# Top-1 expert layers behind attention: what an expert's rows beyond full tiles of 128 are divided into

## The chip, the cores and the metric

One core of a Trainium2 chip. The metric is the device time of one execution in microseconds (us).

## The reference, cut to what matters

```python
# attention: B=4, H=8, S=576, D=64, with a bias from a small network on log(1+|i-j|)/log(i)
x = attn_out.transpose(0, 2, 1, 3).reshape(2304, 512)
logits = normed(x) @ normed(expert_emb).T / tau          # 8 experts
expert_idx = argmax(logits, axis=1)
gate_w = softmax(logits)[arange(2304), expert_idx]
for e in range(8):                                       # F = 1024
    mask = expert_idx == e
    h = maximum(x[mask] @ w1[e], 0.0)
    out[mask] = gate_w[mask, None] * (h @ w2[e])
```

Which rows go to which expert is known only when attention is done, and the experts get very different numbers of rows.

## The kernel before, in words

**Three stages.** Attention runs in 72 units to about 400 us of the span, and each finished tile of 128 rows (18 in all) is routed and written to `xs` in HBM. Then `dispatch` (L1074) plans which rows lie where. Then `moe` (L1273) runs the expert layers.

**Slots.** The expert layers work on slots of 128 rows. A full slot belongs to one expert. What an expert has beyond full slots is rounded up to one part of 64 rows (`half`) or to a full slot, and two 64-row parts of two experts share a slot. Slots 0 to 7 (`EA`) are full ones that `early_slots` (L932) chooses when 15 of the 18 tiles are routed; the rest is planned in `dispatch`: DVE computes counts, prefix sums and comparisons on small tiles, and PE turns them into lists of row numbers (L1135 for full slots, L1160 for 64-row parts). The lists drive GpSimd's indirect DMAs: gather of a slot's rows from `xs` (L1024 early, L1314 later) and scatter of its results (L1303).

**Two programs.** `tc.If` (L1449) chooses by the number of slots used: 21 slots with 3 shared ones (`VAR`, L31), or 22 with 4.

**Expert layers.** F is cut into four quarters q of 256. The first layer of a slot and quarter (`l1`, L1342) is 12 products of 256 columns (f16 high and low halves), the second (`l2`, L1380) 6 products of 512 columns. `product` (L1295) is one matmul with a weight address from a register (the expert's number times its stride) in a full slot (L1298); in a shared slot it is two, on 64 of the array's 128 columns each, L1298 and L1300. Their second expert's weights are copied by DVE beforehand into `wx` (`second`, L1286, L1292), one copy for each layer, quarter and shared slot. ACT and DVE evict the first layer into pairs of slots `h` (three pair buffers), SP transposes a pair into `ht` (L1358), and DVE adds the second layer into `macc` (L1390; L1388 in the first quarter). Weights for the next quarter are loaded (L1246), squared for a scale (ACT L1259, PE L1236) and split into f16 halves (ACT or DVE L1264, DVE L1265) during the layer that doesn't use them; there is one copy of each layer's weights in SBUF.

**Early slots.** The first quarter's first layer of slots 0 to 7 runs inside `dispatch` (`early_x`, `early_h`). `early_act` (L1043) evicts the pairs to the last four slots' rows of `macc`, and four transposes (`early_t`, L1053, issued at L1310) take them to `ht`. A slot whose rows hold such a pair is gathered only after the transpose (token `hr`).

**Order.** `Sched` (L119) simulates engines with a cost for each operation and emits the operations in the order of their simulated starts, each engine in that order. Costs and priorities stand in the `S.op` calls: first layer `100 q + i` in the order of slots (L1283: early, four full ones, shared, the others), second layer `100 q + 21.9 + i`, weights at fractions between. The two programs are planned apart. `dispatch` is written out by hand.

Of the kernel before, what the change touches and what calls it, by code (L numbers as in the profile page):

```python
# [12 lines left out]
I32 = mybir.dt.int32  # L13
# [11 lines left out]
NM = 4  # L25
EXPM = 0x7F800000
# [4 lines left out]
VAR = (21, 3)  # L31
# [225 lines left out]
class Kern:  # L257
# [12 lines left out]
    def setup(self):  # L270
# [34 lines left out]
        self.rc = t("rcst", 293)  # L305
# [4 lines left out]
        self.oh, self.ohs, self.rh = t("oh", NT, E, dt=F16), t("ohs", NT + 1, E, dt=F16), t("rh", NT)  # L310
# [466 lines left out]
    def finish(self, pr, c, xt, prio):  # L777
# [134 lines left out]
        def take():  # L912
# [5 lines left out]
            v.scalar_tensor_tensor(g(6), self.rh[:, ts], -128.0, g(5), ALU.mult, ALU.add)  # L918
            for b in range(nb):
                v.tensor_scalar(self.opt[:, t0 + b], self.iop, g(6)[:, b:b + 1], self.tok[:, t0 + b:t0 + b + 1], ALU.is_equal, ALU.mult)  # L920
# [11 lines left out]
    def early_slots(self, prio):  # L932
# [8 lines left out]
        T = self.early = {a: t("e" + a, *sh, dt=dt) for a, sh, dt in (("cl", [E + 1], F32), ("c", [E], F32), ("be", [n], F32), ("ce", [n], F32), ("es", [EA], F32), ("esi", [EA], I32))}  # L941

        T["ni"], T["f"], T["bt"] = t("ni", E, dt=I32), t("full", E, dt=I32), t("bt", 2, E, E)[:, 0]
        T["tb"], T["os"], T["ge"] = t("tb", NT, E)[:, 0:n], t("os", NT, NB, dt=F16)[:, 0:n, 0:EA], t("ge", NB, E + 1)[:, 0:EA]
# [3 lines left out]
        def init():  # L948
            nc.gpsimd.memset(T["cl"][:, 0:1], 0.0)
            nc.gpsimd.memset(t("base", 2, E + 1)[:, :, 0:1], 0.0)  # L950

# [4 lines left out]
        op("POOL", 130, init, [], [("e", 0)])  # L956
# [38 lines left out]
        def experts():  # L995
# [3 lines left out]
            v.tensor_tensor(self.ohslot[:, 0:EA], T["ge"][:, :, 0:E], T["ge"][:, :, 1:E + 1], ALU.subtract)  # L999

# [42 lines left out]
    def early_act(self, k, part=None):  # L1043
# [3 lines left out]
        pair = lambda k: self.row[:, NS - 1 - k, 0:DM].bitcast(F16).rearrange("p (s d) -> p s d", s=2)  # L1047
# [26 lines left out]
    def dispatch(self):  # L1074
# [19 lines left out]
        full = t("full", E, dt=I32)  # L1094
        ni, fh, bt, base, rj = t("ni", E, dt=I32), t("fh", 2, E, dt=I32), t("bt", 2, E, E), t("base", 2, E + 1), t("rj", 32)
# [7 lines left out]
        v.tensor_scalar(ni, ps[:, 0:E], 63.0, None, ALU.add)  # L1103
# [3 lines left out]
        v.tensor_tensor(more, full, self.early["c"], ALU.subtract)  # L1107
        v.scalar_tensor_tensor(g(6), self.rh[:, l:l + 1], -128.0, g(5), ALU.mult, ALU.add)
# [5 lines left out]
        fsum, hsum, rests = base[:, 0, 1:E + 1], base[:, 1, 1:E + 1], base[:, 1, E:E + 1]  # L1114
# [79 lines left out]
        for k in range(2, EB // 2):  # L1194
            self.early_act(k)
# [273 lines left out]
```

## Time and profile before

| | |
|---|---|
| Median of 3 runs | 685.93 us (684.45 to 686.23) |
| Profiled execution | 688.79 us, span 686.9 us |
| Busy: PE / PE weight load | 619.5 us (90%) / 412.2 us (60%) |
| Busy: DVE / ACT / POOL | 557.7 (81%) / 471.0 (69%) / 174.1 us (25%) |
| DMA | 123.99 MB, mean 181 GB/s |
| Scatters of results (L1303) | 21, POOL, 20.9 us |

The span runs from the first to the last recorded work; the time of the execution is 1.9 us longer. Busy shares are averages over three stages. A matmul's recorded duration includes the pipeline behind its last column, so consecutive matmuls overlap in the records, and the distance between starts is what each costs.

### The profile page before, as it was taken

The page shows a single profiled execution, that of the slowest core. Times are in us where ns is not written, and L with a number is a line of the kernel's source. Part 1 is how long each engine was busy: PE and PEld are TensorE (multiplying, and loading weights), DVE is VectorE, ACT ScalarE, POOL GpSimd, SP SyncE. Part 2 cuts the span into 40 slices and gives each one's busy share as a digit, 9 for nine tenths or more (in the row PEclk, how much of TensorE's full clock was granted, in tenths as well). Part 3 has the DMA queues.
Part 4 walks back from the last instruction along what each step waited for, and adds up shares of the span by engine and source line. Part 5 has one row for each costly group of instructions (what it writes and reads, how often), then busy time and mean ns, then how long its engine had stood idle before and what let it go on. Part 6 is the DMA issues. An engine that isn't in the chain of part 4 may idle for free.

```text
span 686.9 us, 18631 instructions
## 1 busy us (share of the span) xinstructions
PE 619.5 (90%) x6356; PEld 412.2 (60%) x6356; DVE 557.7 (81%) x1573; ACT 471.0 (69%) x1056; POOL 174.1 (25%) x274
## 2 busy tenths in 40 slices
PE   6689999988999888999999877979999999999993
PEld 2345555654667667767677655854675477457641
DVE  6988898888779998999987765948789968987762
ACT  5667687877879887989998446837476647647400
POOL 3555656452221222211210164200000000000073
PEclk9799999999999999999999998989999999999997
DMA  8767646835689946986865459976399549747542
GB/s 247 225 181 218 208 143 188 236 124 164 194 186 278 226 125 153 177 214 190 199 185 130 155 128 268 213 131 194 79 234 218 157 126 233 196 128 162 127 179 100
DMA packets 147842, 123.99 MB, mean 181 GB/s; under 512 B 93830, under 2 KB 122758, under 8 KB 147744
## 3 DMA queue, kind: packets, MB, share of 16 engines
q1 hardware_dynamic: 140256, 96.87, 57.0%
q0 software_dynamic: 7488, 25.85, 11.8%
q8 instruction: 58, 0.95, 0.6%
q14 instruction: 40, 0.33, 0.2%
HBM read 80.70 MB, written 22.29 MB: 150 GB/s over the span
## 4 chain that ended last, share of the span: by engine, by line
PE 37%; issue 35%; DVE 13%; ACT 6%; POOL 4%; DMA 3%; SPq 1%; POOLq 0%; DVEq 0%; ACTq 0%
PE o L737 11%; PE s L685 7%; PE t L716 7%; PE m L630 6%; POOL out L1303 3%; DVE ss L699 3%; ACT pp L702 2%; DVE khl L514 2%; PE o L742 1%; PE m L716 1%; DMA bsc<-stg 1%; DMA macc<-xs,kept 1%; ACT pts L722 1%; PE e L1041 1%; ACT stg L643 1%
## 5 line engine op out<-in xcount | busy, mean ns | idle before, releaser
L1298 PE MATMUL p<-w1s,mxt 128*128 (+1 forms) x912 | 120.2, 276 | 0.1
L702 ACT ACTIVATE pp<-ss,mx 128x576 f32<-128x576 f32 x144 | 112.3, 782 | 11.2 <-DVE mx L699 11.2
L1298 PE MATMUL p<-w2s,mht 128*128 (+1 forms) x504 | 113.9, 379 | 2.7 <-DVE macc L1390 2.4
L699 DVE CUSTOM_DVE_ANT_0 ss<-s,bt 128x576 f32<-128x576 f32 x144 | 104.3, 752 | 11.1 <-PE s L685 9.4
L737 PE MATMUL o<-pts,v 128*64 128x128 f32 x1600 | 105.7, 278 | 3.0 <-DVE xt L754 1.9
L1298 PEld LDWEIGHTS <-mxt 128*128 128x128 f16 (+1 forms) x912 | 88.8, 100 | 24.1 <-issue 3.0
L737 PEld LDWEIGHTS o<-pts,v 128*64 128x64 f32 x1600 | 86.7, 137 | 19.6 <-issue 8.5
L716 PE MATMUL t<-ident,pp 128*128 128x128 f32 x576 | 86.7, 280 | 1.2 <-ACT pp L702 0.4
L1298 PEld LDWEIGHTS <-mht 128*128 128x128 f16 (+1 forms) x504 | 48.7, 99 | 61.4 <-issue 10.4
L685 PE MATMUL s<-kt,qt 64*128 64x512 f16 (+3 forms) x960 | 77.7, 288 | 3.9 <-DVE mx L699 3.0
L1259 ACT ACTIVATE junk<-raw 128x1024 bf16<-128x1024 f32 x50 | 52.7, 1055 | 37.5 <-DMA raw<-in_moe_w 15.7
L722 ACT COPY pts<-t 128x512 f32<-128x512 f32 x121 | 68.1, 589 | 14.0 <-PE t L716 12.6
L1303 POOL DMA_INDIRECT out<-macc,kept x21 | 20.9, 996 | 214.4 <-DVE macc L1390 214.1
L716 PEld LDWEIGHTS t<-ident,pp 128*128 128x128 f32 x576 | 63.5, 141 | 17.6 <-issue 10.0
L617 DVE TENSOR_SCALAR hid<-L,thr 128x576 f32<-128x576 f32 x128 | 65.9, 574 | 9.6 <-PE m L630 9.0
L685 PEld LDWEIGHTS <-qt 64*128 64x128 f16 (+1 forms) x960 | 40.0, 97 | 47.8 <-issue 20.7
L1390 DVE SCALAR_TENSOR_TENSOR macc<-p,aux,macc 128x512 f32<-128x512 f32 x63 | 46.8, 753 | 14.7 <-PE p L1298 13.3
L630 PE MATMUL m<-hid,wt 128*32 128x320 f32 (+1 forms) x488 | 45.3, 423 | 8.7 <-ACT stg L643 3.4
L1352 ACT ACTIVATE h<-p 128x256 f16<-128x256 f32 x70 | 26.0, 378 | 39.0 <-PE p L1298 20.9
L643 ACT ACTIVATE stg<-m,corr 128x256 f32<-128x256 f32 (+1 forms) x88 | 33.7, 418 | 23.5 <-PE m L630 18.9
L1265 DVE SCALAR_TENSOR_TENSOR w1s<-raw,wz,w1s 128x1024 f16<-128x1024 f32 x32 | 40.8, 1278 | 0.1
L1353 DVE SCALAR_TENSOR_TENSOR h<-p,h 128x256 f16<-128x256 f32 x76 | 31.8, 421 | 10.3 <-ACT h L1352 9.8
(323 smaller groups left out, 1046.9 us busy)
## 6 DMA issues: line engine op xcount, KB each, us to landing
raw<-in_moe_w SPq DMA_DIRECT2D x60, 512.0 KB, 4.0
bt<-bsc SPq DMA_DIRECT2D x64, 320.0 KB, 3.5
bsc<-stg POOLq DMA_DIRECT2D x34, 320.0 KB, 3.7
bt<-bsc SPq DMA_DIRECT2D x32, 160.0 KB, 3.4
xs<-row POOLq DMA_DIRECT2D x16, 256.5 KB, 5.6
v<-in_v SPq DMA_DIRECT2D x8, 512.0 KB, 5.4
kr<-in_k SPq DMA_DIRECT2D x8, 512.0 KB, 5.8
q<-in_q SPq DMA_DIRECT2D x8, 512.0 KB, 6.5
```

Source lines behind the costliest of these rows:

```text
L617: e.tensor_scalar(hid(), src[:, off:off + S_], self.thr[:, t0 + x:t0 + x + 1], None, ALU.max)
L630: nc.tensor.matmul(m()[32 * x:32 * x + 32, 0:n], w(x), hx[x]()[:, a:a + n], start=True, stop=True, tile_position=(0, 32 * x))
L685: nc.tensor.matmul(out, lq, k, start=xq + xk == 0, stop=xq == 1, tile_position=(64 * b, 0 if c < 4 else 64 * b))
L699: nc.vector.tensor_tensor_reduce(out=sx(), in0=ss[b]()[:, 448 * b:448 * b + S_], in1=bt()[:, 64 - 64 * b:640 - 64 * b], scale=1.0, scalar= ...
L702: nc.scalar.activation(pp()[:, S_ * b:S_ * b + S_], sx(), AF.Exp, bias=mx()[:, b:b + 1], scale=-1.0, accum_out=sums()[:, h, b:b + 1])
L716: nc.tensor.transpose(t()[:, 128 * k:128 * k + 128], pp()[:, lo + 128 * k:lo + 128 * k + 128], self.ident)
L722: (e.copy if e is nc.scalar else e.tensor_copy)(pts()[:, at:at + n].rearrange("p a b -> p (a b)"), t()[:, 0:128 * n])
L737: nc.tensor.matmul(ob()[64 * b:64 * b + 64, k:k + 128], vv[:, 8 + b if j == 4 else 4 * b + j, :], pts()[:, pb, :], start=j == 0, stop=j == ...
L1259: S.op([("ACT", 1230, lambda: nc.scalar.activation(out() if not own else dst(0), rv() if own else raw(), AF.Square, scale=2.0 ** (-8 if wh ...
L1298: nc.tensor.matmul(out[c, 0:n], lhs[:, c], w[:, bass.ds(ev[s] + at, n)], start=start, stop=stop)
L1303: ins = nc.gpsimd.indirect_dma_start(self.out, bass.IndirectOffsetOnAxis(ap=self.sidx[:, s:s + 1], axis=0), acc[:, s, :], None, bounds_che ...
L1390: S.op([("DVE", 750, lambda a=a, r=r, p2=p2: v.scalar_tensor_tensor(a, p2(), r, a, ALU.mult, ALU.add))], [("p2", q, s), ("rs", q)], [("acc ...
```

## The change

An expert's rest is now a part of 32 rows, always there, and a part of 64 rows where the rest is over 32 (rests over 96 get a full slot). 64-row parts: up to four, in two shared slots, as before. 32-row parts: eight, one for each expert, in two slots of four parts whose experts are fixed (expert 4 s + x at columns 32 x). Slots: 8 early, 2 shared, 2 fixed, 8 others, 20 in all (`NU`). A product in a fixed slot is four matmuls on 32 columns each, with weight addresses known when the program is built, and needs no copy of weights. The early pairs 0 to 2 lie in `ht` at places 8 to 13, no longer in `macc`; only pair 3 lies in the rows of slot 21. If there are more than 8 other slots or more than four 64-row parts, the else-branch computes the former plan anew (`general`) and runs 22 slots.

```diff
-VAR = (21, 3)
+NF = 8
+NU = 8 + NM + NF
...
     def early_act(self, k, part=None):
-        pair = lambda k: self.row[:, NS - 1 - k, 0:DM].bitcast(F16).rearrange("p (s d) -> p s d", s=2)
+        pair = lambda k: (self.ht[:, EB + 2 * k:EB + 2 * k + 2].rearrange("p s b t -> p (s b t)") if k < 3 else self.row[:, NS - 1, 0:DM].bitcast(F16)).rearrange("p (s d) -> p s d", s=2)
...
     def dispatch(self):
-        v.tensor_scalar(ni, ps[:, 0:E], 63.0, None, ALU.add)
+        v.tensor_scalar(ni, ps[:, 0:E], 31.0, None, ALU.add)
...
-        gm, vb, at, hh, thr = t("gm", E), t("vb", E), t("at", E, dt=I32), t("hh", 1), t("thr", E + 1)
-        v.scalar_tensor_tensor(gm, full, -1.25, half, ALU.add, ALU.add)
-        v.tensor_scalar(hh, rests, 0.5, None, ALU.mult)
-        v.tensor_tensor(vb, fsum, hsum, ALU.add)
-        v.tensor_scalar(thr, base[:, 0], hh, None, ALU.add)
-        v.scalar_tensor_tensor(at, vb, hh, gm, ALU.add, ALU.subtract)
+        v.tensor_tensor(at, base[:, 0, 0:E], self.early["ec"], ALU.add)
...
-        for a, b in ((0, NT // 2), (NT // 2, NT)):
-            v.tensor_tensor(os[:, a:b], hp.unsqueeze(1).to_broadcast([128, b - a, NB]), sl[:, a:b].unsqueeze(2).to_broadcast([128, b - a, NB]), ALU.is_equal)
+        v.tensor_tensor(os, hp.unsqueeze(1).to_broadcast([128, NT, NF]), sl.unsqueeze(2).to_broadcast([128, NT, NF]), ALU.is_equal)
...
+        v.tensor_tensor(osh, comb.unsqueeze(1).to_broadcast([128, NT, E + NM]), sl.unsqueeze(2).to_broadcast([128, NT, E + NM]), ALU.is_equal)
+        v.tensor_scalar(esi, em, float(E - 1), 2048.0, ALU.min, ALU.mult)
+        self.used = nc.values_load(used[0:1, :], min_val=0, max_val=32, skip_runtime_bounds_check_because="sum of the slots")
         for j in range(NT):
             for x in range(2):
-                nc.tensor.matmul(ps3[64 * x:64 * x + 64, 0:NM], self.opt[:, j, 0:64], osh[:, j].rearrange("p (s h) -> p h s", h=2)[:, x], start=j == 0, stop=j == l, tile_position=(0, 64 * x))
+                nc.tensor.matmul(ps3[64 * x:64 * x + 64, 0:2], self.opt[:, j, 32:96], osh[:, j, E + 1 - x::2], start=j == 0, stop=j == l, tile_position=(0, 64 * x))
+        for j in range(NT):
+            for x in range(4):
+                nc.tensor.matmul(ps3[32 * x:32 * x + 32, 2:4], self.opt[:, j, 0:32], osh[:, j, x:E:4], start=j == 0, stop=j == l, tile_position=(0, 32 * x))
...
-    def moe(self, aux, ns, nm):
+    def moe(self, aux, ns, quarters):
...
-        a, b = EA + nm, EA + nm + MIX
+        a, b = EA + NM, EA + NM + MIX
         order = [*range(EA), *range(a, b), *range(EA, a), *range(b, ns)]
-        shared, self.order = range(EA, a), order + [*range(ns, NS)]
+        shared, fixed = range(EA, EA + 2 if quarters else a), range(EA + 2, a if quarters else 0)
+        self.order = order + [*range(ns, NS)]
...
         def product(out, lhs, w, s, at, n, b, start, stop):
 
+            for x in range(4) if s in fixed else ():
+                c, e = slice(32 * x, 32 * x + 32), 4 * (s - EA - 2) + x
+                nc.tensor.matmul(out[c, 0:n], lhs[:, c], w[:, 2048 * e + at:2048 * e + at + n], start=start, stop=stop, tile_position=(0, 32 * x))
+            if s in fixed:
+                return
...
-            S.op([("SP", 1244, lambda s=s: self.early_t(s))], [], [("ht", s), ("ht", s + 1), ("hr", NS - 1 - s // 2)], [], HEP, 896, xbar=True)
+            S.op([("SP", 1244, lambda s=s: self.early_t(s))], [("ht", x) for x in (order[EB + s:EB + s + 2] if s < 6 else ())], [("ht", s), ("ht", s + 1), ("hr", NS - 1 if s == 6 else ("x", s))], [], HEP, 896, xbar=True)
...
-        with tc.If(k.used <= VAR[0] - EA) as usual:
-            k.moe(aux, *VAR)
+        with tc.If(k.used <= NF) as usual:
+            k.moe(aux, NU, True)
         with usual.Else():
-            k.moe(aux, NS, NM)
+            k.general(aux)
+            k.moe(aux, NS, False)
```

The rest of the diff in words: `general` holds the former planning, from `gm` and `hh` to the lists, on memory of slots not yet gathered, with the 18 selection tiles `opt` built again; routing flags, ranks and counts (`oh`, `rh`, `pos`, `cnt`, `had`) move to a tile that outlives attention; the constant `rcst` grows by 16 columns (which expert stands in which quarter of a fixed slot), copied by POOL in `early_slots`.

## Rows read from the trace of the kernel before

**Rows 1.** The page, part 1: busy time, share of the span, instructions.

```profile
PE 619.5 (90%) x6356; PEld 412.2 (60%) x6356; DVE 557.7 (81%) x1573; ACT 471.0 (69%) x1056; POOL 174.1 (25%) x274
```

**Rows 2.** Stretches: length, then each engine's busy time, clock, DMA share, GB/s.

```profile
450.00:460.00 10.00, 6.38 (x48) 4.96 (x49) 4.41 (x15) 3.25 (x6) 0.00 (x0) 0.66 0.83 115
520.00:540.00 20.00, 18.61 (x96) 8.95 (x95) 19.65 (x40) 12.80 (x20) 0.00 (x0) 1.00 0.75 186
```

**Rows 3.** Timeline of PE, 482 to 548 us: start, duration, instruction, idle before.

```profile
482.31 7.94 PE L1298 MATMUL p<-w2s,mht 128*128 x36
...
490.09 4.09 PE L1298 MATMUL p<-w1s,mxt 128*128 x36
...
508.06 0.30 PE L1298 MATMUL p<-w1s,mxt 128*64 x1
...
512.87 1.51 PE L1298 MATMUL p<-w1s,mxt 128*128 x12
...
522.92 2.75 PE L1298 MATMUL p<-w2s,mht 128*128 x12
...
547.96 1.47 PE L1298 MATMUL p<-w1s,mxt 128*128 x12
```

**Rows 4.** Timeline of PE, first layer of the last quarter.

```profile
617.49 2.78 PE L1298 MATMUL p<-w1s,mxt 128*128 x24
...
622.86 3.32 PE L1298 MATMUL p<-w1s,mxt 128*128 x24
```

**Rows 5.** Timeline of PE, a shared slot of the first quarter and what follows.

```profile
438.74 0.27 PE L1298 MATMUL p<-w1s,mxt 128*64 x1
438.75 0.27 PE L1300 MATMUL p<-wx,mxt 128*64 128x256 f16 x1
438.85 0.27 PE L1298 MATMUL p<-w1s,mxt 128*64 x1
...
443.53 0.29 PE L1300 MATMUL p<-wx,mxt 128*64 128x256 f16 x1
443.75 4.85 PE L1298 MATMUL p<-w1s,mxt 128*128 x36
```

**Rows 6.** PE and weight loads: bias, lists, shared slots (timelines, source views).

```profile
101.70 0.64 PE L630 MATMUL m<-hid,wt 128*32 128x256 f32 x8 [0.23 <-ACT pts L722]
...
101.67 0.19 PEld L630 LDWEIGHTS m<-hid,wt 128*32 128x32 f32 x8 [0.44 <-issue]
...
L630 PE MATMUL m<-hid,wt x488: 376/432/697, 29.2 to 179.6; 128*32 128x320 f32 x83, 128*32 128x256 f32 x80
...
411.40 0.76 PE L1160 MATMUL t<-osh,opt 128*64 128x4 f16 x36
...
L1300 PEld LDWEIGHTS <-mxt x144: 106/106/110, 438.5 to 638.4; 128*64 128x64 f16 x144
```

**Rows 7.** DVE: copies for shared slots (source view), last weight splits (timeline).

```profile
L1292 DVE COPY wx<-w1s x12: 682/688/696, 426.9 to 636.1; 128x2048 f16 x12
...
520.27 1.28 DVE L1265 SCALAR_TENSOR_TENSOR w2s<-raw,wz,w2s 128x1024 f16<-128x1024 f32 x1
...
546.53 1.28 DVE L1265 SCALAR_TENSOR_TENSOR w1s<-raw,wz,w1s 128x1024 f16<-128x1024 f32 x1
```

**Rows 8.** Timelines of POOL, DVE, PE: end of quarter one's first layer.

```profile
438.80 1.49 POOL L1314 DMA_INDIRECT macc<-xs,kept  x1 [15.88 <-ACT w2s L1264]
...
453.30 0.42 DVE L1352 TENSOR_SCALAR h<-p 128x256 f16<-128x256 f32 x1 [7.81 <-DMA mht<-h]
...
455.50 4.87 PE L1298 MATMUL p<-w1s,mxt 128*128 x24
...
461.57 5.34 PE L1298 MATMUL p<-w2s,mht 128*128 x24
```

**Rows 9.** Timelines of PE and POOL in the planning.

```profile
415.47 0.62 PE L1034 MATMUL e<-id,macc 128*128 128x128 f16 x8 [1.00 <-DMA macc<-xs,kept]
...
410.69 0.98 POOL L1314 DMA_INDIRECT macc<-xs,kept  x1 [1.44 <-DVE esi L1174]
```

More of the change, by code (lines that the diff above doesn't have):

```diff
@@ new lines, in dispatch @@
+        for j in range(NT):
+            for x in range(4):
+                nc.tensor.matmul(ps3[32 * x:32 * x + 32, 2:4], self.opt[:, j, 0:32], osh[:, j, x:E:4], start=j == 0, stop=j == l, tile_position=(0, 32 * x))
+        self.early_x(5)
+        self.early_h(3)
+        self.early_x(6)
+        self.early_x(7)
+        self.early_act(1, False)
+        for s in range(4, EB):
+            self.early_h(s)
+        _, ev = nc.values_load_multi_w_load_instructions(esi[0:1, 2:NM + NF], engines=(mybir.EngineType.PE,), min_val=0, max_val=7 * 2048, skip_runtime_bounds_check_because="an expert's number times its stride")
@@ new lines, in dispatch @@
+        self.ev = [*self.ev, *ev[0:2], None, None, *ev[2:]]
+        v.tensor_tensor(self.ohslot[:, EA + NM:NU], ge[:, :, 0:E], ge[:, :, 1:E + 1], ALU.subtract)
+        for x in range(2):
+            r = slice(64 * x, 64 * x + 64)
+            v.tensor_copy(self.ohslot[r, EA:EA + 2], eq.rearrange("p (s h) e -> p h s e", h=2)[r, 1 - x])
+        v.tensor_scalar(self.gidx[:, EA:EA + NM], ps3[:, 0:NM], float(HOLE), None, ALU.add)
+        self.drops(NU, lambda n: t(n, NS))
+        _, self.ev2 = nc.values_load_multi_w_load_instructions(esi[0:1, 0:2], engines=(mybir.EngineType.DVE,), min_val=0, max_val=7 * 2048, skip_runtime_bounds_check_because="an expert's number times its stride")
@@ new lines, in dispatch, with drops @@
+        self.early_act(0, True)
+        self.early_act(1, True)
+        for k in range(2, EB // 2):
+            self.early_act(k)
+    def drops(self, ns, t):
+        v, gall = self.nc.vector, self.gidx[:, 0:ns]
+        pad, one = t("pad")[:, 0:ns], t("one")[:, 0:ns]
+        v.tensor_scalar(pad, gall, float(HOLE), 8192.0, ALU.is_equal, ALU.mult)
+        v.scalar_tensor_tensor(one, gall, float(HOLE), pad, ALU.is_gt, ALU.subtract)
+        self.sidx = self.kept[:, NS:2 * NS].bitcast(I32)
+        v.tensor_tensor(self.sidx[:, 0:ns], gall, one, ALU.subtract)
@@ L1313, in moe @@
                 continue
-            S.op([("POOL", 1038, lambda s=s: nc.gpsimd.indirect_dma_start(row[:, s, 0:DM + 1], None, self.xs, bass.IndirectOffsetOnAxis(ap=(self.gidx if s not in shared else self.gall.bitcast(I32))[:, s:s + 1], axis=0)))], [("hr", s)], [("g", s), ("acc", s)], [], i - GL, 734)
+            S.op([("POOL", 1038, lambda s=s: nc.gpsimd.indirect_dma_start(row[:, s, 0:DM + 1], None, self.xs, bass.IndirectOffsetOnAxis(ap=self.gidx[:, s:s + 1], axis=0)))], [("hr", s)], [("g", s), ("acc", s)], [], i - GL, 734)
             if XD0 <= i < XD1:
@@ L1426, in host_arrays @@
     rc[:, 229:293] = (np.arange(E)[None, :] <= np.arange(E)[:, None]).reshape(-1)
+    for e in range(E):
+        rc[32 * (e % 4):32 * (e % 4) + 32, 293 + E * (e // 4) + e] = 1
     a["rcst"] = rc
```

142 lines of the change are left out of this document (89 added, 53 removed).

## The prediction

> **What bounds the kernel now.** I read the page first, then the busy times by stretch, then TensorE's timeline. The page has PE busy for 90% of the span [rows 1]; that is an average over attention, the planning of the slots and the expert layers, and the change touches only the last two. In the expert layers the stretches show PE at 18.6 of 20 us even where DVE is at its fullest (19.65 of 20) [rows 2], so PE paces them with DVE a close second. The reader should see in the timeline of the second quarter how regular it is: first layer from 490.09 to 522.92 (32.83 us, 18 full slots and 3 shared), second layer from 522.92 on [rows 3]. The three shared slots take 508.06 to 512.87, 4.81 us or 1.60 each; the rest is 28.02 us, 1.56 per full slot. The second layer costs 1.30 per slot: six slots (36 matmuls) between 482.31 and 490.09 [rows 3].
>
> Two paces matter. Full slots of the first layer run at 2.78 us per 24 matmuls straight after a second layer and at 3.32 later [rows 4]: the array could do about 0.11 us per matmul, but the stream of instructions with an address in a register does not keep up for long. The two 64-column tiles of a shared slot start 0.01 apart, and the next pair 0.11 after them [rows 5], so two tiles cost what one full matmul costs.
>
> **Does the new layout fit the inputs?** Counting the reference's own routing gives 4, 1, 583, 115, 554, 28, 291 and 728 rows per expert. Parts of 128 with up to 64 + 32 left over give 4+1+4+2+5 = 16 full slots and four 64-row parts (583, 554, 291, 728). Early planning takes 8 slots, so 8 remain and the two shared slots are full: exactly the limit of the 20-slot branch. The nearest margin is two rows (291 = 256 + 35, the limit of a 32-row part being 32), and its loss would only free a part.
>
> **The change part by part.**
> *First layer, quarters two to four.* Before: 28.02 + 4.81 = 32.83. After: 16 full slots at 1.557 = 24.9; two shared at 1.60 = 3.2; two of four tiles. No expert-layer row shows four f16 tiles. The nearest are the f32 bias matmuls: eight matmuls on four 32-column tiles fill 0.64 us, though one alone lasts 0.376 at the least, and their eight weight loads fill 0.19 together [rows 6]. So four tiles do load and run side by side. Issue is no obstacle: 36 load-and-matmul pairs with fixed addresses take 0.76 us, 0.021 each, so four cost 0.084, below 0.11 [rows 6]. A four-tile product therefore costs 0.11 as a pair does, 12 of them 1.32. The bounds: 0.084 with the array out of the way (1.0 per slot, and the saved issue time passed to the full slots behind it), and for the upper end the shared slots' own 1.60. I take 1.32, the pair being the same operation on twice the columns.
> One more change of tile width comes with it (128, 64, 32, 128 instead of 128, 64, 128). Behind the last pair the next full matmul starts 0.22 later [rows 5], where pairs are 0.11 apart, so a change costs 0.1. Sum: 24.9 + 3.2 + 2.64 + 0.1 = 30.85, which is 1.95 less; three times, **-5.9**.
> *Second layer, all four quarters.* One slot of 1.30 less, four-tile slots at the pace of the others (four issues of 0.021 lie far below 0.216 per product), 0.1 for the change of width: -1.2, four times **-4.8**.
> The Trainium skill, page TensorEngine Tiling (Array Packing), section Tiling Modes, says that a change of tiling mode drains TensorE, whereas a change of tile alone doesn't. That speaks against this change, and the 0.22 us above agrees with it; were the drain free, the sum would be 0.7 lower (seven passes of 0.1).
> *First quarter, start.* Its last three first-layer slots run from 455.50 to the second layer's start at 461.57; the first two fill 4.87 of that, so the third took 1.2 [rows 8], and one goes: **-1.2**. Two slots took 4.87 because the granted clock of this stretch was 0.66, a mixture of the levels 1.2 and 2.4 GHz, behind a wait of PE [rows 2]. That wait (PE has filled its PSUM tiles, and DVE waits 7.81 us for a transpose to land before it may refill an h buffer [rows 8]) I leave where it is: that transpose still stands in SP's queue behind the four early ones. What changes around it: three late gathers (the first at 438.80, after 15.88 us of idle POOL, because the early h pairs lay in their rows [rows 8]) become two early ones, as the pairs move to ht. A gather's issue takes 0.98 early on and 1.49 at 438.80 [rows 8, 9]: two ahead of the early transposes may push them by some 2.0, and without the three up to 1.49 + 2 x 0.98 = 3.4 of crowded DMA goes from behind them. Both ends stay in the range; I take 0. The new dependency, that a pair's place in ht is refilled only when its early transpose has read it, queues on SP behind the same transposes, so I cost it at nothing; the cover is SP's order.
> *Planning.* DVE loses some nine small operations and gains a few; PE gains 72 tiny matmuls, 72 x 0.021 = 1.5 us. They stand before the transposes of the last early slots, where PE waits 1.00 us for a gather [rows 9]; 0.5 would show. POOL's first late gather waits 1.44 us for the experts' numbers [rows 9], which come over 1 us sooner. I take 0, with +0.5 and -1.1 as ends. A wider constant, a 16-column copy on POOL and a larger else-branch: nothing, since POOL idles in attention and the branch isn't entered.
> *Copies of second weights.* Eight of 24 DVE copies of 0.69 us go (in each layer 12, three slots in four quarters [rows 7]; now two slots). They lie beside PE's matmuls, so 0; but in three second layers DVE is full [rows 2], and there up to 3 x 0.69 = 2.1 could come back.
> *Gathers and scatters.* One each less. The last scatter still follows the last slot, so the end moves with PE and nothing further is won.
>
> Sum: -5.9 - 4.8 - 1.2 = **-11.9**. The profiled execution took 688.79 (span 686.9), 2.9 above the median of the runs, 685.93. The change's profiled execution should take 676.9, the median run **674.0**.
>
> **Rivals.**
> *Weight preparation sets the stages (13%).* It is the same work for 20 slots as for 21. The last write of the second layer's weights ends at 521.55, 1.37 before the second layer starts; the last of the first layer's ends at 547.81, 0.15 before that layer's next start at 547.96 [rows 3, 7]. If preparation keeps its pace, the first layer can win 1.37 of 1.95 (three times: -4.1), second layers one to three nothing, the last -1.2, the start -1.2: -6.5, 679.4. Against: its operations stand on DVE between the evictions and move up with them, and where preparation ends at 547.81, 25 us into the second layer, only some 19 of its 21 slots can have run at 1.30, so matmuls are left to do.
> *The four tiles run two at a time (6%), slower.* Place: the products of the two fixed slots. Then 12 x 0.11 and 6 x 0.216 come on top per slot and quarter: 2 x 4 x 2.62 = +21, so 685.93 - 11.9 + 21.0 = 695.0. It decides from 1.5 us more per fixed slot and quarter on (11.9 / 8). Against it: the bias rows [rows 6], whose stationary operand has the same shape, though in f32.
> A milder form is that loads queue behind matmuls: 18 products x 0.106 x 8 = +15.3, 689.3. The Trainium skill, page TensorE: Matmul & The Clock Gate, section The mechanism, has such a rule: a weight load overlaps running matmuls only in other row groups, and all four tiles use all rows. The pairs [rows 5, 6] use all rows as well, load for 0.106 and still follow at 0.11, so the trace disagrees; that form has 1 of the 6%.
> *The change isn't what it says (2%).* With one full slot or part more than counted, the else-branch plans anew and runs 22 slots: one more slot (4 x 2.86 = +11.4) and some 60 DVE operations of 0.2 to 0.3 us after planning (about +14): 711.
> *The gain is swallowed (3%)* by the first quarter's transposes and a less fortunate order of the planner: within the bounds above, no change.
>
> **How the numbers follow.** Forecast 76%. Low end: -11.9 with -1.6 (three times 0.54, two full slots at the faster pace [rows 4]), -2.1, -3.4 and -1.1 gives 666; the four together are unlikely, so 667. High end: +2.0 at the start, +0.5 planning, and fixed slots at 1.60 in three quarters (+1.7) give 678.2; the first rival 679.4. Range 667 to 681. Faster by over 0.3% (2.1 us, about what a measurement of this kernel can tell from no change): 76 + 13 = 89%; within: 4%; slower: 7%.
>
> **What would show it.** In the profile after: 20 scatters; the first layer of the second quarter at 30.9 us instead of 32.8; four-tile products 0.11 apart in the first layer and 0.216 in the second; the second layer of the first quarter starting near 460. Wrong: four tiles 0.2 apart, PE idle ahead of a second layer behind w2s, or a longer wait before 455.

## The result, and the profile after

| | before | after |
|---|---|---|
| median of the runs | 686.08 us (684.45 to 689.07, 4 runs) | 678.47 us (677.85 to 678.93, 4 runs) |
| profiled execution (span) | 688.79 us (686.9) | 677.85 us (676.1) |

The ratio is 0.9884, with a 95% interval of 0.9848 to 0.9919: the kernel became faster, by 7.6 us between the medians and by 10.9 us between the two profiled executions. The forecast was 674.0 for the median and 676.9 for the profiled execution, the range 667 to 681. Both measured times lie inside; the median is 4.5 above its forecast, the profiled execution 1.0 above its own.

I read the same views in the same order. Part 1 of the page of after, which answers to [rows 1]:

```profile
PE 608.5 (90%) x6708; PEld 406.7 (60%) x6708; DVE 543.1 (80%) x1540; ACT 471.9 (70%) x1056; POOL 172.0 (25%) x273
```

PE loses 11.0 us of work and DVE 14.6, and PE is still busy for 90%: the saving is work of PE, not a wait. The two stretches of [rows 2], after:

```profile
450.00:460.00 10.00, 8.26 (x93) 6.21 (x86) 5.25 (x14) 4.53 (x10) 0.00 (x0) 0.83 1.14 192
520.00:540.00 20.00, 18.59 (x99) 8.77 (x99) 19.59 (x41) 14.53 (x23) 0.00 (x0) 1.00 0.75 200
```

In a second layer DVE is as full as before (19.59 of 20), with PE at 18.59. The end of the first quarter's first layer now has PE at 8.26 of 10 instead of 6.38. The timeline of PE in the second quarter, to set against [rows 3]:

```profile
480.50 2.77 PE L1372 MATMUL p<-w2s,mht 128*32 128x512 f16 x48
...
488.40 4.09 PE L1376 MATMUL p<-w1s,mxt 128*128 x36
...
509.90 1.50 PE L1372 MATMUL p<-w1s,mxt 128*32 128x256 f16 x48
...
511.44 1.50 PE L1372 MATMUL p<-w1s,mxt 128*32 128x256 f16 x48
514.15 0.16 PE L1308 MATMUL st<-wz,onesb 128*128 128x1 bf16 x1 [1.22 <-ACT junk L1331]
514.24 3.28 PE L1376 MATMUL p<-w1s,mxt 128*128 x24
...
520.45 2.83 PE L1376 MATMUL p<-w2s,mht 128*128 x11
```

Here is the change itself. One fixed slot is 48 matmuls, four for each of 12 products, in 1.50 us. The last matmul lasts 0.27 of it, so the products are (1.50 - 0.27) / 11 = 0.112 apart: four tiles cost what one full matmul costs. In the second layer two fixed slots are 48 matmuls in 2.77, which is (2.77 - 0.38) / 11 = 0.217 per product. The source view of that line gives the operations singly (minimum, median and maximum, in ns):

```profile
L1372 PEld LDWEIGHTS <-mxt x384: 92/97/98, 448.5 to 631.7; 128*32 128x32 f16 x192
L1372 PE MATMUL p<-w1s,mxt x384: 272/273/284, 448.5 to 631.8; 128*32 128x256 f16 x192
```

The wait at 514.15 is new: ahead of a product for a weight's scale (st) PE stands 1.22 us for ScalarE (junk), which itself waited 2.35 us for a raw weight to land. In the kernel before, such waits come to 0.35 us in the three first layers together. The last quarter's first layer, to set against [rows 4]:

```profile
609.83 2.78 PE L1376 MATMUL p<-w1s,mxt 128*128 x24
...
615.12 2.78 PE L1376 MATMUL p<-w1s,mxt 128*128 x24
...
617.77 3.27 PE L1376 MATMUL p<-w1s,mxt 128*128 x24
```

The quick pace of 2.78 per 24 matmuls now holds for 72 matmuls, where before it was gone at the third group or sooner. Copies for shared slots [rows 7] are 16 instead of 24. The end of the first quarter's first layer, which answers to [rows 8]:

```profile
457.00 3.61 PE L1376 MATMUL p<-w1s,mxt 128*128 x24
...
460.47 1.46 PE L1376 MATMUL p<-w2s,mht 128*128 x6
```

The second layer starts at 460.47 instead of 461.57. Last, the planning. DVE's timeline in the kernel before had the branch number (used) ahead of the list's eviction:

```profile
407.80 0.16 DVE L1144 TENSOR_TENSOR used<-hh,most 128x1 int32<-128x1 f32 x1
...
408.30 0.17 DVE L1150 TENSOR_SCALAR kept<-m 128x14 int32<-128x14 f32 x1
```

After, it stands behind it:

```profile
409.97 0.17 DVE L1142 TENSOR_SCALAR kept<-m 128x8 int32<-128x8 f32 x1 [2.25 <-PE m L1132]
...
410.15 0.15 DVE L1145 SCALAR_TENSOR_TENSOR used<-base 128x1 int32<-128x1 f32 x1
```

The eviction waits 2.25 us for PE's list, and the branch number with it: 2.35 us later than before, though the first early transposes run only 0.72 later (402.55 and 403.27). Not all of the rest is the order. PE's list came later as well, because the first early products took longer, before and after:

```profile
404.39 1.69 PE L1041 MATMUL e<-w1s,mxt 128*128 x12 [0.68 <-ACT mxt L1035]
405.10 2.64 PE L1045 MATMUL e<-w1s,mxt 128*128 x12
```

These 0.95 us are PE's granted clock, 1.00 from 403 to 407 us in before and 0.64 in after, a mixture of its two levels, 1.2 and 2.4 GHz; what made it fall is not shown, and the kernel before has the lower clock there too in one run (0.74, experiment 8). Where the changed kernel kept a clock of 1.00 in that stretch (experiments 6 and 7), the branch number is ready 5.9 us behind the first early transposes, against 5.25 in before and 6.9 here. So the order by itself costs some 0.65 us, and more the later the list is. All engines need that number to enter the branch, and POOL's first late gather moves from 410.69 [rows 9] to 412.72.

To find where the time went I cut the span at four kinds of instruction: the first early transposes (e<-id), the first matmul of each second layer (w2s), the start of each following first layer (w1s), and the last scatter. In the third and the fourth quarter one first-layer slot runs ahead of the last slots of the second layer (four of them in before, two in after):

```profile
547.23 1.47 PE L1376 MATMUL p<-w1s,mxt 128*128 x12
548.54 2.75 PE L1376 MATMUL p<-w2s,mht 128*128 x12
551.13 2.78 PE L1376 MATMUL p<-w1s,mxt 128*128 x24
```

That slot, 1.3 us each time, counts with the second layers here, and the first layer starts behind it (551.13). The kernels with 21 slots and with late loads have no such slot: to set one of them against another row, 2.6 us have to be moved from its first layers to its second layers. "Start" is from the first early transposes to the first quarter's second layer; the first layers are those of quarters two to four, the second layers all four, the last one up to the last scatter. About 9.4 to 9.7 us follow. Every profiled execution of this study is in the table. Rows of one letter are from one batch; B, C and D are three different chips. Medians and ratios in this document leave out executions over 1.5% above the fastest of the same kernel, and the two rows marked * are such executions.

| profile | first e | start | three first layers | four second layers | span |
|---|---|---|---|---|---|
| before, A | 402.55 | 59.02 | 32.83 + 31.41 + 30.88 = 95.1 | 120.6 | 686.9 |
| after, A | 403.27 | 57.20 | 32.05 + 28.18 + 29.26 = 89.5 | 116.6 | 676.1 |
| before again, B | 410.21 | 62.12 | 94.6 | 124.9 | 701.6 |
| after again, B | 403.04 | 61.72 | 92.4 | 119.9 | 686.6 |
| branch number first, B | 402.92 | 59.52 | 90.3 | 121.6 | 683.9 |
| pairs in macc, B | 400.71 | 59.52 | 92.1 | 120.5 | 682.3 |
| both edits, C * | 404.38 | 58.65 | 91.5 | 116.7 | 680.7 |
| 21 slots, C | 405.18 | 58.28 | 33.77 + 33.55 + 31.97 = 99.3 | 121.8 | 694.2 |
| light loads, after, C | 403.64 | 53.51 | 85.7 | 115.2 | 667.5 |
| light loads, before, C | 403.88 | 53.24 | 93.4 | 118.5 | 678.6 |
| after a third time, D | 404.13 | 58.49 | 31.75 + 28.59 + 30.49 = 90.8 | 117.4 | 680.3 |
| branch number again, D * | 404.52 | 59.99 | 93.1 | 117.0 | 684.1 |
| late loads, D | 404.82 | 52.15 | 32.13 + 31.94 + 31.66 = 95.7 | 118.7 | 681.0 |
| fixed addresses, D | 403.17 | 55.83 | 30.42 + 28.57 + 28.86 = 87.9 | 117.9 | 674.3 |

From before to after in batch A: start -1.1 net of the first e (-1.8 from it), first layers -5.6, second layers -4.0, tail -0.1, together -10.8.

### The profile page after: what moved, and what is told of

The parts are those of the page before. It is cut to its first block, busy times and chain, and to the rows that moved or that the text cites. A ratio compares the mean times of both kernels' runs of the same rounds, so it can differ in the third digit from the quotient of the medians.

```text
span 676.1 us, 19064 instructions
## 1 busy us (share of the span) xinstructions
PE 608.5 (90%) x6708; PEld 406.7 (60%) x6708; DVE 543.1 (80%) x1540; ACT 471.9 (70%) x1056; POOL 172.0 (25%) x273
## 4 chain that ended last, share of the span: by engine, by line
PE 37%; issue 35%; DVE 10%; DMA 6%; ACT 6%; POOL 4%; SPq 1%; POOLq 0%; ACTq 0%; DVEq 0%
PE o L738 12%; PE s L686 7%; PE t L717 7%; PE m L631 6%; DMA macc<-xs,kept 4%; POOL out L1381 3%; DVE ss L700 3%; ACT pp L703 3%; DVE khl L515 2%; PE o L743 1%; PE m L717 1%; ACT pts L723 1%; DMA bsc<-stg 1%; DMA kr<-in_k 1%; ACT stg L644 1%
## 5 line engine op out<-in xcount | busy, mean ns | idle before, releaser
L738 PE MATMUL o<-pts,v 128*64 128x128 f32 x1600 | 107.9, 282 | 3.0 <-DVE xt L755 1.8
L1376 PE MATMUL p<-w1s,mxt 128*128 (+1 forms) x768 | 99.7, 276 | 1.9 <-issue 1.7
L738 PEld LDWEIGHTS o<-pts,v 128*64 128x64 f32 x1600 | 88.6, 139 | 20.0 <-issue 8.0
L1376 PE MATMUL p<-w2s,mht 128*128 (+1 forms) x432 | 97.5, 379 | 2.7 <-DVE macc L1468 2.3
L1376 PEld LDWEIGHTS <-mxt 128*128 128x128 f16 (+1 forms) x768 | 74.8, 100 | 22.3 <-issue 4.9
L1381 POOL DMA_INDIRECT out<-macc,kept x20 | 19.7, 986 | 217.9 <-DVE macc L1468 217.9
L1376 PEld LDWEIGHTS <-mht 128*128 128x128 f16 (+1 forms) x432 | 41.3, 99 | 53.1 <-issue 8.7
L1468 DVE SCALAR_TENSOR_TENSOR macc<-p,aux,macc 128x512 f32<-128x512 f32 x60 | 44.5, 752 | 13.4 <-PE p L1376 9.9
L1430 ACT ACTIVATE h<-p 128x256 f16<-128x256 f32 x65 | 24.2, 376 | 32.2 <-PE p L1376 17.4
L1431 DVE SCALAR_TENSOR_TENSOR h<-p,h 128x256 f16<-128x256 f32 x72 | 30.1, 421 | 14.7 <-ACT h L1430 14.2
```

Source lines behind the costliest of these rows:

```text
L738: nc.tensor.matmul(ob()[64 * b:64 * b + 64, k:k + 128], vv[:, 8 + b if j == 4 else 4 * b + j, :], pts()[:, pb, :], start=j == 0, stop=j == ...
L1376: nc.tensor.matmul(out[c, 0:n], lhs[:, c], w[:, bass.ds(ev[s] + at, n)], start=start, stop=stop)
L1468: S.op([("DVE", 750, lambda a=a, r=r, p2=p2: v.scalar_tensor_tensor(a, p2(), r, a, ALU.mult, ALU.add))], [("p2", q, s), ("rs", q)], [("acc ...
```

## Experiments

**1 and 2. Both kernels unchanged, on chip B.** No edit.

> The kernel before, unchanged, to see how far its own executions lie apart and where. The profile of before that the sum was made against took 688.79 us, 2.7 above the median. Theory: the 2.7 lie in the first quarter's start (about 400 to 462 us of the span), where transposes and gathers share the DMA queues, and this profile, if it is nearer to 686, shows the second layer of the first quarter starting 1 to 3 us before 461.6 and stage lengths from there on within 0.5 us of the first profile's. Rival: the excess lies in the first layers of quarters two to four (weights landing late), then the start is within 0.5 us of 461.6 and a first layer is 1 us or more shorter. Ratio 1.000 within 0.003.

> The changed kernel, unchanged, for a closer ratio and a second profile. The sum of the prediction (-11.9) says a ratio of 0.983; the first runs say 0.988 (-7.6). Theory: 0.986 to 0.989, since the profile of before was one of its slow executions. Rival: the true difference is the sum's and the first runs were unlucky, 0.983.

Before again: 697.15 us (694.48 to 703.41, 13 runs), ratio to before in the same batch 0.9993 (0.9971 to 1.0015). After: 688.63 us (687.97 to 689.53, 6 runs), ratio 0.9879 (0.9846 to 0.9912), 8.8 us faster. This chip takes 11 us longer for the same kernel, and the gain is the same: the second theory holds, and its rival's 0.983 lies outside the interval. The profile of before is its slowest execution, 6 us above its median, so it can't tell where the 2.7 us of the first expectation lie; of its 15.0 us over after's, 7.2 lie ahead of the first early transposes, in attention, which the change does not touch. A difference between two profiles has to be read stage by stage, as in the table.

**3. The branch number first.** In after, one line moves up, so that DVE computes `used` before it waits for the list:

```diff
+        ch, used, esi = t("ch", NM, E), t("used", 1, dt=I32), t("esi", NM + NF, dt=I32)
+        v.scalar_tensor_tensor(used, base[:, 1, E:E + 1], float(NF - NM), base[:, 0, E:E + 1], ALU.add, ALU.max)
         v.tensor_scalar(self.gidx[:, EA + NM:NU], ps2[:, 0:NF], float(HOLE), None, ALU.add)
         v.tensor_tensor(cm, eq, comb[:, 0:E].unsqueeze(1).to_broadcast([128, NM, E]), ALU.mult)
-        ch, used, esi = t("ch", NM, E), t("used", 1, dt=I32), t("esi", NM + NF, dt=I32)
-        v.scalar_tensor_tensor(used, base[:, 1, E:E + 1], float(NF - NM), base[:, 0, E:E + 1], ALU.add, ALU.max)
```

> The changed kernel with one line moved: the number of slots that decides the branch is computed before, not after, the operation that waits for PE's list of full slots. In the profile after, that number was ready at 410.3 (before: 408.0), SP's first load of the branch was issued at 411.2 (before: 408.8) and POOL's first late gather at 412.7 (before: 410.7). Theory (the branch of every engine waits for this number, and the change put it 2.3 us later): SP's load and the gathers come 1.5 to 2.5 us earlier, the second layer of the first quarter starts 1 to 2 us earlier, and the whole is 0.5 to 2 us faster than the changed kernel (ratio to before 0.984 to 0.988). Rival (POOL is held by the experts' numbers or by its own earlier gathers): the gathers move by less than 0.5 us and the time stays, as the gathers land in a full DMA queue anyway.

Measured: 684.93 us (683.41 to 687.43, 6 runs), ratio 0.9825 (0.9788 to 0.9862), 3.7 less than after on the same chip; no run of the one reaches a run of the other. DVE's timeline, with the number 4.4 us ahead of the eviction:

```profile
407.30 0.15 DVE L1143 SCALAR_TENSOR_TENSOR used<-base 128x1 int32<-128x1 f32 x1
411.67 0.17 DVE L1144 TENSOR_SCALAR kept<-m 128x8 int32<-128x8 f32 x1 [4.22 <-PE m L1132]
```

SP's first weight load inside the branch comes at 409.79 instead of 412.95, POOL's first late gather at 412.10 instead of 414.48, and the second layer of the first quarter 59.5 us behind the first early transposes instead of 61.7. So on this chip after did lose time in the planning, where the prediction had 0, and more than the theory's 0.5 to 2.

**4. The pairs back in macc.** In after, the early h pairs lie in the rows of late slots again, as they did before:

```diff
-        pair = lambda k: (self.ht[:, EB + 2 * k:EB + 2 * k + 2].rearrange("p s b t -> p (s b t)") if k < 3 else self.row[:, NS - 1, 0:DM].bitcast(F16)).rearrange("p (s d) -> p s d", s=2)
+        pair = lambda k: self.row[:, NS - 1 - k, 0:DM].bitcast(F16).rearrange("p (s d) -> p s d", s=2)
...
-            S.op([("SP", 1244, lambda s=s: self.early_t(s))], [("ht", x) for x in (order[EB + s:EB + s + 2] if s < 6 else ())], [("ht", s), ("ht", s + 1), ("hr", NS - 1 if s == 6 else ("x", s))], [], HEP, 896, xbar=True)
+            S.op([("SP", 1244, lambda s=s: self.early_t(s))], [], [("ht", s), ("ht", s + 1), ("hr", NS - 1 - s // 2)], [], HEP, 896, xbar=True)
```

> The changed kernel with the early pairs back in the rows of the last four slots, and the gathers of slots 18 and 19 again behind their transposes; all else as changed. Theory of the prediction (the move of the pairs is worth nothing by itself, within -3.4 to +2.0): the time stays within 1.5 us of the changed kernel's. Rival (without late gathers the transposes land sooner, and this is where the start's 1.1 us came from): 1.5 to 3.5 us slower, the wait of PE before the last first-layer slots back at 6 to 7 us.

Measured: 686.72 us (684.18 to 688.92, 6 runs), ratio 0.9858 (0.9822 to 0.9895), 1.9 less than after. The intervals overlap, so the size is open, but there is no sign that moving the pairs helped: the theory allowed 1.5 either way, the rival had the other sign, and the 1.9 are near the loss of 2.0 that the prediction had kept as its upper end.

**5. Both edits together, on chip C.**

> The kernel after, with two edits: the branch number is computed ahead of the gather list's eviction on DVE (as in the run with that edit alone, which was 3.7 us faster than after), and the early h pairs lie in the rows of the last four late slots again with gathers 18 and 19 behind the transposes (1.9 us faster alone). Theory: the two act at different places, one on the branch and the first late gather, the other on the gathers ahead of the early transposes, so they add: 688.6 - 3.7 - 1.9 = 683.0, second layer of the first quarter 59.4 us or less after the first early transposes instead of 61.7, ratio to before 0.979. Rival: both shorten one and the same wait of the first quarter (PE out of h tiles), so only the larger one shows: 684.9 to 685.5, ratio 0.983.

Measured: 678.35 us (671.5 to 680.83, 5 runs), ratio 0.9867 (0.9818 to 0.9915). The sum of the two gains, 0.979, lies outside the interval; the rival's 0.983 lies in it, and so does after's own ratio. The runs lie 9 us apart, so all that can be said is that there is no sign of the two gains adding up. The start of 58.65 has no profile of after on this chip to be set against.

**6. 21 slots in the new division.** The price of one slot, by adding an empty one to after:

```diff
-NF = 8
+NF = 9
```

> The kernel after with nine places for full slots of the late kind instead of eight, so that 21 slots run, one of them empty, with the shared slots still divided into two of two and two of four parts. Nothing of the computation is left out. It prices one slot. Theory: the slot alone was worth 11 us (three first layers at 1.56, one at 1.2 behind the wait, four second layers at 1.30) and after lost some 3 us of it in the planning, because the branch number comes later: then this kernel is slower than before by about 3, ratio 1.003 to 1.006, and 11 us slower than after. Rival: a slot is worth only what the change showed, 8.4 us, because weights and DVE set part of the stages: then it is level with before, ratio 0.998 to 1.002.

Measured: 696.11 us (693.12 to 697.83, 6 runs), ratio 1.0134 (1.0096 to 1.0172): 9.4 slower than before with its 21 slots, and with after at 0.984 to 0.988 some 17 to 21 us dearer than after. Both forecasts missed. The table says where: against the third profile of after (chip D), with the 2.6 us moved, the first layers cost 5.9 more instead of 4.7 and the second layers 7.1 more instead of the 5.2 of four times 1.30. In the second layers PE stands 4.3 us at scale products (2.6 of them at 530.40), in after 1.0. In the third quarter's first layer, by the timeline of PE:

```profile
580.12 2.58 PE L1372 MATMUL p<-w1s,mxt 128*32 128x256 f16 x86
583.31 0.51 PE L1372 MATMUL p<-w1s,mxt 128*32 128x256 f16 x10 [0.60 <-issue]
584.36 0.16 PE L1308 MATMUL st<-wz,onesb 128*128 128x1 bf16 x1 [0.55 <-ACT junk L1331]
584.45 3.37 PE L1376 MATMUL p<-w1s,mxt 128*128 x24
```

PE pauses twice around the fixed slots and then goes at the slow pace, as at 514.15 in after. At an equal count of slots this kernel is slower than the old division, so by this run the whole gain of the change is the slot. But it is no clean price of a slot: the planner's order changed with it (no first-layer slot runs ahead), and why the pauses are longer than before (1.9 us at scale products in the three first layers and 4.3 in the second layers, against 0.35 and 0.6) is not settled, as chip, order and division differ at once.

**7 and 8. Light loads.** In both kernels the same edit of the raw weight loads:

```diff
-... nc.sync.dma_start(rv(), src.rearrange("(k p) f -> p k f", p=128))
+... nc.sync.dma_start(rv()[:, 0:1] if q else rv(), src.rearrange("(k p) f -> p k f", p=128)[:, 0:1] if q else src.rearrange("(k p) f -> p k f", p=128))
```

> The kernel after with the raw weight loads of quarters two to four cut to their first part (a quarter of each first-layer block, half of each second-layer block); the rest of each block keeps what an earlier load left, so those weights are not the real ones. All instructions of the engines stay. Theory: in the first layers of quarters two to four PE stands 3.7 us in all at a weight-scale product that waits for ScalarE and for a raw weight that lands late; with short loads these waits go and the kernel takes 684 to 686, against 688.6 of after. Rival: the wait is for the raw buffer to come free (DVE's split of the weight before), not for the transfer: then nothing changes, 688 to 689.

> The kernel before with the same cut of the raw weight loads (same weights not the real ones). Theory: its first layers hardly wait for raw weights (0.3 us in all), so it gains under 1 us, and the difference between before and after grows from 8.5 to 11 or more with light loads. Rival: the loads crowd something else in both kernels alike, so both gain the same and the difference stays at 8 to 9.

After: 667.02 us (665.31 to 669.32, 4 runs), ratio 0.9712 (0.9669 to 0.9754). Before: 681.98 us (679.63 to 685.25, 10 runs), ratio 0.9942 (0.991 to 0.9973). The difference grows to 15.0, as the theory had it (11 or more), and more of it than expected goes to after: against the ratio of 0.984 to 0.988 that it has with whole loads, 8 to 12 us, where the waits seen at the scale products on chip B were 3.7. Before gains 4.0 by its ratio, where its theory had under 1. The rival of the first run, that nothing changes, and that of the second, that both gain the same, are refuted. By the table the first layers of after fall to 85.7, with no wait at a scale product left, and the start falls to 53.5 in both kernels. So the weights' transfers are nearer to the bound in after than in before. I read it so that the slot that went had been time in which they landed; no run shows that by itself.

**9 and 10. After, and the branch number first, a second time on chip D.**

> The kernel after, unchanged, on the chip of this batch, as the yardstick for the three others and as a third measurement of the change. Theory: 0.988 of before as on the two chips so far (0.9884, 0.9879). Rival: the gain depends on the chip or the hour, then it lies outside 0.983 to 0.993.

> The kernel after with the branch number ahead of the gather list's eviction, a second time, since the run with this and the pairs' edit together came out at 0.9867 with a wide spread. Theory: the branch number 2.5 to 3 us earlier is worth 3 to 4 us in the end, ratio 0.980 to 0.985, and 3 us less than after in this batch. Rival: the first quarter waits for the transposes of the early h tiles anyway, so it is worth nothing: level with after, 0.988.

After: 678.77 us (676.55 to 682.11, 6 runs), ratio 0.9835 (0.9797 to 0.9873), 10.6 faster than before and at the edge of the 0.983 to 0.993 that the theory allowed. The branch number first: 677.69 us (675.07 to 681.54, 5 runs), ratio 0.9827 (0.9784 to 0.9869), 1.1 less than after where the theory had 3. The sign is that of run 3, the size is not, and here the intervals overlap nearly whole: the edit gains something between 0 and 4. Of the versions that use the real weights it has the best medians in both batches, and it is the one I would keep, with that reservation. DVE's timeline gives a reason for the two sizes. On chip B the eviction waits 4.2 us for PE's list, in after on chip D only 1.7:

```profile
410.64 0.17 DVE L1142 TENSOR_SCALAR kept<-m 128x8 int32<-128x8 f32 x1 [1.72 <-PE m L1132]
410.83 0.15 DVE L1145 SCALAR_TENSOR_TENSOR used<-base 128x1 int32<-128x1 f32 x1
```

With the edit the branch number is ready 4.4 us behind the first early transposes on both chips, without it 8.9 on B and 6.7 on D, so there is less to win on D. SP's first load moves from 411.86 to 409.94 there. The profiles of the two decide nothing on the start (59.99 * and 58.49).

**11. Late loads.** Run 3, and the second quarter's first weight loads made to wait for the fourth h transpose of the first quarter:

```diff
-... ["w1pool" if not first or e < 2 else ("eg", EGL)] + (held if part == 1 else []), [t], [raw], prio, 1460)
+... ["w1pool" if not first or e < 2 else ("eg", EGL)] + (held if part == 1 else []) + ([("ht", self.order[15])] if (which, q) == (1, 1) else []), [t], [raw], prio, 1460)
```

> The branch number first, and the raw loads of the second quarter's first-layer weights wait until the fourth of the first quarter's six transposes of new h tiles has been issued; in after four of these loads (2 MB) go just ahead of the transposes. With short loads the second layer of the first quarter started 53.5 us after the first early transposes, in before and after alike, against 58 to 62. Theory: these four loads are what the transposes meet, so the second layer starts at 54 to 57 behind the first early transposes and the kernel takes 2 to 4 us less than with the branch number first alone, ratio 0.976 to 0.981. Rival: the loads come too late for the second quarter's first layer, PE waits for w1s ahead of it, and the time is the same or up to 5 us longer.

Measured: 683.1 us (680.38 to 688.25, 10 runs), ratio 0.9897 (0.9866 to 0.9929): 4.3 slower than after and 5.4 slower than the branch number first alone, and the transposes went earlier all the same. SP's queue in after (third profile), with 4 raw loads between the early transposes and those of new h tiles:

```profile
438.05 4.11 SPq L1057 DMA_TRANSPOSE mht<-macc  x1
442.27 3.95 SPq L1318 DMA_DIRECT2D raw<-in_moe_w  x4
446.56 18.39 SPq L1436 DMA_TRANSPOSE mht<-h  x6
```

and in this kernel:

```profile
436.96 3.45 SPq L1057 DMA_TRANSPOSE mht<-macc  x1
441.20 14.84 SPq L1436 DMA_TRANSPOSE mht<-h  x5
456.09 1.70 SPq L1318 DMA_DIRECT2D raw<-in_moe_w  x3
```

The h transposes start 5.4 earlier, at the same 3.0 us each, and the start shrinks from 58.5 to 52.2, beyond the theory's 54 to 57. All of it is given back: with the 2.6 us moved (this plan has no first-layer slot that runs ahead), first layers +2.3 and second layers +4.0. PE's waits in the second layers grow from 4.7 to 7.7 us, 1.7 of it at scale products; that the weights come later by what was won is my reading of it. The waits of PE show none for w1s ahead of the second quarter's first layer, so the rival had the total about right and the place wrong. Why the third quarter's first layer loses 2.0 and the first quarter's second layer 1.8 stays open; the planner's order differs too.

**12. Fixed addresses.** In after, constants instead of registers in the products of full slots and first tiles:

```diff
-... w[:, bass.ds(ev[s] + at, n)], start=start, stop=stop)
+... w[:, 2048 * (s % E) + at:2048 * (s % E) + at + n] if quarters else w[:, bass.ds(ev[s] + at, n)], start=start, stop=stop)
```

> The kernel after with constant instead of register addresses in the products of the full slots and of the first tile of the shared ones: each slot then takes the weights of expert (slot mod 8), not those of its own. All matmuls, loads and waits stay. Theory: the pace of 0.137 us per matmul in the first layers is the stream of register instructions, not the array, so at constant addresses they run at 0.11: first layers of quarters two to four at 27 to 28 us instead of 29 to 32, ratio 0.970 to 0.978. Rival: the weights' preparation sets the first layers' length; then PE waits longer at the weight-scale products and the stages shorten by under 1 us each, ratio 0.984 to 0.988.

Measured: 675.9 us (673.78 to 678.75, 4 runs), ratio 0.9801 (0.9749 to 0.9853), between the two theories, 2.9 less than after. Its timeline of PE shows that both were half right:

```profile
555.96 2.78 PE L1376 MATMUL p<-w1s,mxt 128*128 128x256 f16 x24
...
567.39 1.49 PE L1372 MATMUL p<-w1s,mxt 128*32 128x256 f16 x48
570.51 0.16 PE L1308 MATMUL st<-wz,onesb 128*128 128x1 bf16 x1 [1.62 <-ACT junk L1331]
570.53 2.78 PE L1376 MATMUL p<-w1s,mxt 128*128 128x256 f16 x24
```

Every group of 24 now takes 2.78, (2.78 - 0.27) / 23 = 0.109 per matmul, also behind a wait. But PE now stands 3.1, 2.5 and 3.0 us at scale products in the three first layers, so that they shrink by 3.0 in all (90.8 to 87.9) and not by the 8.5 that they would without the longer waits. Compare after (third profile), where the pace depends on what went before:

```profile
575.45 2.84 PE L1376 MATMUL p<-w1s,mxt 128*128 x24
...
578.81 0.16 PE L1308 MATMUL st<-wz,onesb 128*128 128x1 bf16 x1 [0.53 <-ACT junk L1331]
578.90 3.29 PE L1376 MATMUL p<-w1s,mxt 128*128 x24
```

Straight behind the fixed slots 24 matmuls take 2.84; behind a wait, 3.29. The issue time that a fixed slot saves is passed on to the full slots behind it, as the lower bound of the prediction had supposed, but only if no wait stands between. For the quick pace there this rests on two places, this one and 573.20 in the first profile of after (2.99).

## Why the prediction was right, point by point

*That 20 slots run:* right, with 20 scatters (L1381, 19.7 us) instead of 21.

*That four tiles cost what a pair costs:* right. 0.112 and 0.217 us per product, forecast 0.11 and 0.216. The rival in which they run two at a time (+21 us) is refuted, and so is its milder form. The Trainium skill, page TensorE: Matmul & The Clock Gate, section The mechanism, lists (its opening lines are wider) that a weight load overlaps running matmuls only in another row group, by which these loads would queue behind matmuls, since all four tiles use all rows; this trace disagrees, with loads of 0.097 us and products 0.112 apart.

*The change of width, 0.1:* about right. In the second layer the full matmul at 483.21 starts 0.32 behind the last four-tile product (480.50 + 2.77 - 0.38), 0.10 more than the 0.217 of the others. The Trainium skill, page TensorEngine Tiling (Array Packing), section Tiling Modes, says that a change of tiling mode drains TensorE; this trace agrees that a change of tile size costs something.

*First layers, -5.9:* measured -5.6 between the profiles of batch A, but not as 32.83 to 30.85 three times. With the slot that runs ahead counted in (1.31), they took 32.05, 29.49 and 30.57, so the three saved 0.8, 3.2 and 1.6 where 1.95 was forecast. I had taken one mean pace for full slots, 1.557, and no new wait. The runs show two paces: in the second quarter, where no slot runs ahead, the quick one holds for the same 36 matmuls (4.09 us) before and after, and a wait of 1.2 us at a scale product is new; in the third and the fourth it lasts longer than before, for a reason that no run shows. The size of the term is right by luck, since these two errors cancelled.

*Second layers, -4.8:* measured -4.0, so the term was oversized by 0.8. PE's waits in the four second layers grew by 1.1, from 2.9 to 4.0 us: for DVE's accumulations (macc) from 2.3 to 2.8, with new ones around the fixed slots (0.16 at 538.35, 0.38 at 543.22), at scale products from 0.6 to 0.8, and 0.4 for a scale (wz). The price of a slot there, 1.30, is not confirmed by run 6, where it came to 1.8 with the longer waits.

*Start of the first quarter, -1.2:* measured -1.1, within a stretch that scatters more than that. The same kernel after started its second layer 57.2, 61.7 and 58.5 us behind its first early transposes in three batches. The one number agrees with the forecast; it doesn't confirm the slot's 1.2 by itself, since the next point lies in it too, and the late gathers that went, for which run 4 shows no gain.

*Planning, 0 with +0.5 and -1.1 as ends:* wrong in sign. The step that failed is "the experts' numbers come over 1 us sooner": I counted operations and not their order. The experts' numbers (esi) start at 411.00 instead of 410.50, 0.2 sooner if counted from the first early transposes. The branch number had been computed ahead of a wait for PE's list and now comes behind it, 2.35 us later, of which the order by itself is some 0.65. Moving it back ahead gained 3.7 in one batch and 1.1 in another.

*Weight preparation sets the stages (rival, 13%):* refuted as stated, since the second layers one to three won 0.6, 0.9 and 1.1 us, where it allowed nothing. As a bound it lies closer than I had it. Light loads and fixed addresses show both sides: with a quicker PE the waits at scale products grow by 5.5 us (3.1 to 8.6) where first layers shrink by 3.0, and with quicker weights the difference between the two kernels grows from about 9 to 15.

*From the profiled execution to the median:* the sum was -11.9, the profiled pair gave -10.9, the medians -7.6, -8.8 and -10.6 in three batches. The profile of before was 2.7 above its median, that of after 0.6 below its own. I had carried a difference from one execution over to the median whole; the runs of before alone lie 684.45 to 689.07, and the table shows the start stretch and the pace of first layers changing from one execution of a kernel to the next. The median could not be had closer than that.

## What to carry to other kernels

When a plan is rewritten, look not only at how many operations go but at which value is computed behind which wait: a number that every engine needs belongs ahead of an eviction that waits for another engine. Price a removed unit of work from the stage it leaves, and then ask what stood beside it: here, as I read the runs, the slot also gave the weights time to land, and part of the next gain (fixed addresses, and perhaps late loads) was swallowed by just that. Compare two executions by stage, and by the stretch that the change does not touch, before believing a difference of 3 us, and check that both plans put the same slots into the stage.

## What the hardware showed that I had not expected

The slow pace of matmuls with an address in a register has a visible companion on the load queue of PE. The source view of L1376 in after:

```profile
L1376 PEldq FUSED_REGOPS  x1200: 42/46/46, 429.4 to 661.6; - x172
L1376 PEld LDWEIGHTS <-mxt x768: 94/97/151, 430.1 to 638.7; 128*128 128x128 f16 x168, 128*64 128x64 f16 x24
```

There are 1200 such instructions of 46 ns, one for each of the 768 + 432 products of that line. A load of 97 ns and one of these together make 0.143 us; the slow pace is (3.29 - 0.27) / 23 = 0.131. With constant addresses the rows are gone (the page counts 17,864 instructions instead of 19,064, 1200 fewer) and the pace is 0.109 throughout. In the second layers, at 0.217 per product, they hide. That the two add up on one queue is my reading of these numbers, not shown by a run of its own; their sum lies above the pace, so they can't follow each other whole.

Batches on different chips differ more than this change is worth: before takes 686.1, 697.5, 686.7 and 689.4 us in the medians of four batches, while the ratio of after to before stays within 0.9835 and 0.9884.
